# The first pair of heads in an attention and gated-MLP kernel: its loads on two queues and its parts made head by head

## The chip, the cores and the metric

The kernel runs on one core of a Trainium2 chip. The metric is the device time of one execution in microseconds (us). TensorE does the matrix products and the transposes, VectorE, ScalarE and GpSimd the elementwise work, and DMA transfers are issued here by the queue of SyncE (the sync queue).

## The reference

Attention over 2 batches of 12 heads, 448 positions, head size 64, then two layers on the 896 rows of 768 that come out of it.

```python
scores = scale * np.matmul(q, k.transpose(0, 1, 3, 2))     # causal mask, softmax
attn_out = np.matmul(attn, v)
x = attn_out.transpose(0, 2, 1, 3).reshape(B * S, H * D)
g = x @ w_gate                                             # 768 -> 1536
x = (g * sigmoid(g) * (x @ w_val)) @ w_out                 # 1536 -> 768
h = x @ w_in                                               # 768 -> 2048
out = (h * np.clip(h + 3, 0, 6) / 6) @ w2_out              # 2048 -> 768
```

The weights come as float64. The kernel makes float32 of them on the chip, and splits operands into a rounded high part and a remainder, so that the fast float32r products keep enough digits.

## The kernel before

Attention runs first, the two layers after it. Heads go in twelve pairs. For a pair, keys and queries are loaded as they lie (112 positions on the partitions, four chunks, two heads side by side), and `turn_parts` turns them on TensorE so that the 64 numbers of a position lie on the partitions: head 0 of the pair in rows 0 to 63, head 1 in rows 64 to 127. Scores are two products over 128 rows: one with the keys' high part (`kk`) in both halves, one with the keys' remainder (`k2`) in both halves, and the queries (`qq`) with their high part in one half and their remainder in the other. A turned half thus has to come into the other half as well. For pairs from the second on, ScalarE copies the turned block (L261), VectorE casts (L268), GpSimd makes the remainder (L269), and the sync queue copies each half of the keys to the other half by DMA (L274).

The first pair has a path of its own, `first_turn` (L278). Four transposes of the keys and four of the queries (L285), of both heads at once; then per head (`head`) two VectorE steps for the keys (L297, L298), ScalarE's cast of the queries (L299), a GpSimd and a ScalarE copy to the other half (L300, L302), and VectorE's remainder of the queries (L301). Head 0 is made at once, head 1 in the middle of round 0.

The rounds of L455 are one per head. Round t holds the scores and softmax of head t (`sc_parts`: products L330, VectorE L343, ScalarE L353), the transposes of the exponentials of head t-1 (`tp_parts`, L373), the value products of head t-2 (`pv_parts`, L401), and in even rounds the turns of the next pair, in odd ones the transposes of a finished pair. `weave` mixes the lists evenly. `busy(n)` puts n filler products on zeros (L194) on TensorE; the five numbers of `IDLE` (L31) say how many go where: at the start, behind the key transposes, behind the query transposes, in round 0, in round 1.

The order on an engine is not the written one throughout: a planner orders the instructions with costs of its own, in the written order where all is ready by its reckoning, and puts ready work ahead of work that it holds not ready. An instruction under `tc.keep_in_program_order` stays behind the one written before it on its engine; before, of TensorE's only the fillers do. Each engine then runs its list in order. Eight banks of PSUM are handed round by the list `idle`.

## Time and profile before

| | |
|---|---|
| median of 3 runs | 621.32 us (621.04 to 621.56) |
| the profiled execution | 619.02 us, span 617.2 us |
| TensorE busy | 607.9 us (98%), 3618 products |
| VectorE busy | 344.4 us (56%) |
| ScalarE busy | 264.7 us (43%) |
| GpSimd busy | 186.0 us (30%) |
| DMA | 70.15 MB, mean 114 GB/s |

The span runs from the first to the last instruction of the profiled execution; all positions below are microseconds from its start. PE is TensorE, PEld its weight load, DVE VectorE, ACT ScalarE, POOL GpSimd, SPq the sync queue. A product's length in the timeline includes its way through the array, so products that follow one another overlap; the distance of their starts is what each costs. L285 is line 285 of the kernel.

### The profile page before, as it was taken

Reading aid. Unit: us, or ns where it says so; the run is one execution under the profiler, and the core shown is the slowest. Engines: PE = TensorE matmul, PEld = TensorE weight load, DVE = VectorE, ACT = ScalarE, POOL = GpSimd, SP = SyncE. Lnnn points to the kernel's source line nnn. Section 1 sums busy time; section 2 is a strip of 40 time slices with the busy share of each in tenths; the row PEclk is TensorE's granted clock in tenths of the full one; section 3 lists DMA queues with packets and bytes.
Section 4 is the critical chain, followed back from the end, with each engine's and each line's share of the span. In section 5 each row is a group of like instructions: output and inputs, shape, how many; then the busy total and the mean of one; then the engine's idle time right before and its main releaser. Section 6 shows DMA issues by size and latency. Waiting matters only on the chain.

```text
span 617.2 us, 9392 instructions
## 1 busy us (share of the span) xinstructions
PE 607.9 (98%) x3618; PEld 561.8 (91%) x3618; DVE 344.4 (56%) x688; ACT 264.7 (43%) x450; POOL 186.0 (30%) x125
## 2 busy tenths in 40 slices
PE   8999998999999999999999999999999999999997
PEld 5999998988999988888999888889998899999996
DVE  6888889859854455554443444665656653325101
ACT  5687777744433333333323323555455532232100
POOL 4555665125222222222222222222222222213200
PEclk9999999999999999999999999999999999999999
DMA  9855543146443333333333333333343333352002
GB/s 184 226 138 132 138 110 97 58 150 201 157 125 127 108 102 103 102 103 103 117 124 115 105 103 102 104 102 108 111 132 111 102 103 103 102 180 65 0 4 88
DMA packets 83917, 70.15 MB, mean 114 GB/s; under 512 B 35232, under 2 KB 79776, under 8 KB 83872
## 3 DMA queue, kind: packets, MB, share of 16 engines
q1 hardware_dynamic: 83872, 69.55, 38.9%
q8 instruction: 29, 0.48, 0.3%
q14 instruction: 16, 0.13, 0.1%
HBM read 61.73 MB, written 2.75 MB: 104 GB/s over the span
## 4 chain that ended last, share of the span: by engine, by line
PE 94%; DVE 3%; ACT 1%; DMA 0%; issue 0%; SPq 0%; DVEq 0%; ACTq 0%
PE mm L170 60%; PE mm L547 19%; PE pv L401 5%; PE sc L330 4%; PE tp L373 3%; PE tr L255 1%; PE tr L435 1%; DVE e L343 1%; DVE qq L268 0%; DMA qn<-in_q_dram 0%; DVE w L102 0%; DVE w L105 0%; ACT e L353 0%; PE zero L194 0%; ACT whi L110 0%
## 5 line engine op out<-in xcount | busy, mean ns | idle before, releaser
L111 POOL TENSOR_TENSOR wlo<-w,whi 128x768 fp32r<-128x768 f32 x68 | 128.1, 1884 | 356.0 <-ACT whi L110 293.6
L101 DVE TENSOR_SCALAR w<-w 128x768 uint32<-128x768 uint32 x68 | 38.8, 570 | 155.9 <-ACT w L98 155.7
L110 ACT CAST whi<-w 128x768 fp32r<-128x768 f32 x68 | 56.9, 837 | 124.4 <-PE mm L170 82.8
L170 PE MATMUL mm<-x1l,whi 128*128 128x384 f32 (+1 forms) x288 | 104.9, 364 | 0.2 <-DVE x1l L153 0.2
L98 ACT ACTIVATE w<-raw 128x768 f32<-128x768 f32 x68 | 61.1, 898 | 102.1 <-POOL wlo L111 98.5
L170 PE MATMUL mm<-x1h,wlo 128*128 128x384 f32 (+1 forms) x288 | 104.9, 364 | 0.0
L170 PE MATMUL mm<-x1h,whi 128*128 128x384 f32 (+1 forms) x288 | 104.5, 363 | 0.0
L105 DVE SCALAR_TENSOR_TENSOR w<-raw,w 128x768 uint32<-128x768 uint32 x68 | 74.5, 1096 | 1.0
L547 PE MATMUL mm<-whi,gl 128*128 128x384 f32 x224 | 74.8, 334 | 0.0
L547 PE MATMUL mm<-whi,gh 128*128 128x384 f32 x224 | 74.8, 334 | 0.0
L547 PE MATMUL mm<-wlo,gh 128*128 128x384 f32 x224 | 74.8, 334 | 0.0
L401 PE MATMUL pv<-v,et 112*112 112x65 f32 x480 | 73.5, 242 | 0.0
L170 PE MATMUL mm<-x2h,wlo 128*128 128x384 f32 (+1 forms) x192 | 70.0, 364 | 0.0
L170 PE MATMUL mm<-x2l,whi 128*128 128x384 f32 (+1 forms) x192 | 69.8, 364 | 0.0
L170 PE MATMUL mm<-x2h,whi 128*128 128x384 f32 (+1 forms) x192 | 69.6, 362 | 0.0
L401 PEld LDWEIGHTS pv<-v,et 112*112 112x112 f32 x480 | 65.8, 177 | 1.2
L102 DVE SCALAR_TENSOR_TENSOR w<-raw,w 128x768 uint32<-128x768 uint32 x68 | 65.8, 968 | 1.6
L373 PE MATMUL tp<-ident,e 112*112 112x112 f32 x240 | 61.1, 261 | 3.1 <-ACT e L353 2.9
L170 PEld LDWEIGHTS mm<-x1l,whi 128*128 128x128 f32 x288 | 54.0, 188 | 6.5 <-DVE x1l L153 0.5
L170 PEld LDWEIGHTS mm<-x1h,whi 128*128 128x128 f32 x288 | 54.1, 188 | 6.2 <-ACT x1h L152 0.3
L170 PEld LDWEIGHTS mm<-x1h,wlo 128*128 128x128 f32 x288 | 54.0, 188 | 5.6
L353 ACT ACTIVATE e<-e,m 112x336 f32<-112x336 f32 (+1 forms) x96 | 48.6, 530 | 20.7 <-DVE m L343 20.6
(72 smaller groups left out, 1049.6 us busy)
## 6 DMA issues: line engine op xcount, KB each, us to landing
raw<-in_moe_w_out_dram SPq DMA_DIRECT2D x28, 768.0 KB, 4.3
raw<-in_moe_w_in_dram SPq DMA_DIRECT2D x16, 768.0 KB, 4.5
raw<-in_moe_w_gate_dram SPq DMA_DIRECT2D x12, 768.0 KB, 4.2
raw<-in_moe_w_val_dram SPq DMA_DIRECT2D x12, 768.0 KB, 4.3
kn<-in_k_dram SPq DMA_DIRECT2D x24, 112.0 KB, 2.8
qn<-in_q_dram SPq DMA_DIRECT2D x24, 112.0 KB, 2.7
v<-in_v_dram SPq DMA_DIRECT2D x12, 224.0 KB, 3.3
out_dram<-ob SPq DMA_DIRECT2D x14, 192.0 KB, 1.8
```

What stands on the lines that cost most here:

```text
L98: first = nc.scalar.activation(out=w, in_=high.bitcast(F32), func=AF.Copy, scale=2.0**-112)
L101: nc.vector.tensor_scalar(out=wu, in0=wu, scalar1=3, scalar2=None, op0=ALU.logical_shift_left)
L102: nc.vector.scalar_tensor_tensor(out=wu, in0=high, scalar=0x80000000, in1=wu, op0=ALU.bitwise_and, op1=ALU.bitwise_or)
L105: nc.vector.scalar_tensor_tensor(out=wu, in0=low, scalar=29, in1=wu, op0=ALU.logical_shift_right, op1=ALU.bitwise_or)
L110: nc.scalar.copy(hi, w)
L111: nc.gpsimd.tensor_tensor(out=lo, in0=w, in1=hi.bitcast(F32), op=ALU.subtract)
L170: lambda lhs=lhs, rhs=rhs, i=i: nc.tensor.matmul(ps, lhs, rhs, start=(first and i == 0), stop=(last and i == total - 1))
L330: nc.tensor.matmul(sp[:C, o : o + w], t["qq"][:, j, c * C : (c + 1) * C], t[("kk", "k2")[i]][:, j, 0:w], start=(i == 0), stop=(i == 1),)
L353: nc.scalar.activation(out=es, in_=es, func=AF.Exp, scale=-1.0, bias=m[:, x : x + 1])
L373: nc.tensor.transpose(tp[:C, at - lo : at - lo + C], e[:, at : at + C], ident[:C, :C])
L401: nc.tensor.matmul(box["o"][:, qc, :], et[:, at : at + C], vt[:, j, c, :], start=(c == 0), stop=(c == qc))
L547: nc.tensor.matmul(acc, lhs[:, tsl], rhs[:, i, :], start=(fc == 0 and n == 0), stop=(fc == K2 - 1 and n == 2),)
```

## The change

- Six loads take the place of `load(0)`: the keys of head 0 twice, side by side (`twice[0]`), the queries of heads 0 and 1, and the keys of head 1 twice. The first of each pair of loads goes to the sync queue, the other to ScalarE's queue. `load(1)` follows on the sync queue.
- The transposes are made head by head: keys 0, a filler, queries 0 (only the first 64 columns), a filler, queries 1, keys 1, two fillers: 16 transposes where there were 8. A transpose of doubled keys leaves them in both halves of its bank.
- Per head, ScalarE casts the keys for all 128 rows at once and VectorE makes their remainder for all 128; the copies to the other half are gone. The queries are made as before. Both heads are made ahead of round 0.
- Round 0 is written as the eight score products alone, then the eight turns of the second pair woven with three fillers. Round 1 begins with the first two score products of head 1; its other parts and two fillers are woven. The turns of the second pair and the scores of head 1 are kept in program order.
- `IDLE` goes from 6, 1, 3, 6, 2 to 5, 1, 1, 2, 3, 2.

```diff
-IDLE = (6, 1, 3, 6, 2)
+IDLE = (5, 1, 1, 2, 3, 2)
...
+                    if p == 1:
+                        tc.keep_in_program_order(turn)
...
             def first_turn():
                 t = sets[0]
-                got = {}
-                for nm, src in (("k", natk), ("q", natq)):
-                    got[nm] = bank("tr")
+                kb = [bank("tr") for _ in range(2)]
+                qb = [bank("tr") for _ in range(2)]
+
+                def keys(j):
                     for c in range(NC):
                         nc.tensor.transpose(
-                            got[nm][0][:, c * C : (c + 1) * C],
-                            src[0][:, c].rearrange("p j d -> p (j d)"),
+                            kb[j][0][:, c * C : (c + 1) * C],
+                            twice[j][:, c].rearrange("p j d -> p (j d)"),
                             ident[:C, :C],
                         )
-                    busy(IDLE[1] if nm == "k" else IDLE[2])
-                kt, qt = (got[nm][0][:, :S] for nm in "kq")
+
+                def queries(j):
+                    n = D * (j + 1)
+                    for c in range(NC):
+                        nc.tensor.transpose(
+                            qb[j][0][:n, c * C : (c + 1) * C],
+                            natq[0][:, c].rearrange("p j d -> p (j d)")[:, :n],
+                            ident[:C, :C],
+                        )
 
                 def head(j):
...
-                    nc.vector.tensor_copy(kk[r], kt[r])
-                    nc.vector.tensor_tensor(out=k2[r], in0=kt[r], in1=kk[r].bitcast(F32), op=ALU.subtract)
+                    kt, qt = (x[j][0][:, :S] for x in (kb, qb))
+                    nc.scalar.copy(kk, kt)
                     nc.scalar.copy(qq[r], qt[r])
-                    nc.gpsimd.tensor_copy(kk[o], kk[r].bitcast(F32))
+                    nc.vector.tensor_tensor(out=k2, in0=kt, in1=kk.bitcast(F32), op=ALU.subtract)
                     nc.vector.tensor_tensor(out=qq[o], in0=qt[r], in1=qq[r].bitcast(F32), op=ALU.subtract)
-                    nc.scalar.copy(k2[o], k2[r].bitcast(F32))
...
+                keys(0)
+                busy(IDLE[1])
+                queries(0)
+                busy(IDLE[2])
+                queries(1)
+                keys(1)
+                busy(IDLE[3])
                 head(0)
-                return [lambda: head(1)]
+                head(1)
...
+                    if n == 1:
+                        tc.keep_in_program_order(score)
...
-            load(0)
+            twice = [fix.tile([C, NC, 2, D], F32, name=f"twice{j}") for j in range(2)]
+            natq[0] = nat.tile([C, NC, 2, D], F32, tag="qn", name="qn")
+            def fetch(queue, dst, src):
+                queue.dma_start(out=dst, in_=src.rearrange("(c p) d -> p c d", p=C))
+            fetch(nc.sync, twice[0][:, :, 0, :], k[0, 0])
+            fetch(nc.scalar, twice[0][:, :, 1, :], k[0, 0])
+            fetch(nc.sync, natq[0][:, :, 0, :], q[0, 0])
+            fetch(nc.scalar, natq[0][:, :, 1, :], q[0, 1])
+            fetch(nc.sync, twice[1][:, :, 0, :], k[0, 1])
+            fetch(nc.scalar, twice[1][:, :, 1, :], k[0, 1])
             load(1)
             load_v(0)
-            second = first_turn()
+            first_turn()
...
-                fill = [lambda: busy(1)] * (IDLE[3 + t] if t < 2 else 0)
-                weave(sc_parts(t), tp_parts(t - 1), pv_parts(t - 2), turns_now, second, fill)
+                if t == 0:
+                    weave(sc_parts(t))
+                    weave(turns_now, [lambda: busy(1)] * IDLE[4])
+                    continue
+                fill = [lambda: busy(1)] * (IDLE[5] if t == 1 else 0)
+                scores = sc_parts(t)
+                if t == 1:
+                    weave(scores[:2])
+                    scores = scores[2:]
+                weave(scores, tp_parts(t - 1), pv_parts(t - 2), turns_now, fill)
```

## Rows read from the trace of the kernel before

**Rows 1.** busy time by stretch (start:end, length; per engine busy, instructions; then clock, DMA)
```profile
7.89:10.81 2.92, 1.77 (x12) 1.36 (x11) 2.67 (x10) 2.19 (x6) 2.25 (x2) 1.00 1.35 214
...
14.05:18.60 4.55, 4.55 (x44) 4.46 (x45) 2.83 (x12) 3.29 (x8) 2.08 (x2) 1.00 0.99 266
18.60:27.50 8.90, 8.80 (x88) 8.48 (x87) 7.62 (x29) 6.32 (x15) 5.08 (x5) 1.00 0.87 220
```

**Rows 2.** waits of TensorE over the span (us in total, times, longest)
```profile
PE tp L373 <- ACT e L353: 2.9, 3, 1.6
```

**Rows 3.** timeline of TensorE (start, length, what, idle before and its releaser)
```profile
1.19 2.74 PE L194 MATMUL zero<-zeros 128*128 128x512 bf16 x6 [1.19 <-DVE half L523]
3.72 0.76 PE L285 MATMUL tr<-ident,kn 112*128 112x112 f32 x4
...
5.11 0.57 PE L285 MATMUL tr<-ident,qn 112*128 112x112 f32 x4 [0.41 <-DMA qn<-in_q_dram]
5.52 0.81 PE L194 MATMUL zero<-zeros 128*128 128x512 bf16 x3
6.17 0.29 PE L255 MATMUL tr<-ident,kn 112*128 112x112 f32 x1
...
7.89 0.38 PE L330 MATMUL sc<-kk,qq 128*112 128x336 f32 x1
...
10.81 0.31 PE L373 MATMUL tp<-ident,e 112*112 112x112 f32 x1 [1.15 <-ACT e L353]
...
14.05 0.31 PE L373 MATMUL tp<-ident,e 112*112 112x112 f32 x1 [0.20 <-ACT e L353]
...
14.65 0.39 PE L330 MATMUL sc<-k,qq 128*112 128x336 f32 x1
```

**Rows 4.** timeline of VectorE
```profile
4.51 0.62 DVE L297 CAST kk<-tr 64x448 fp32r<-64x448 f32 x1 [3.34 <-PE tr L285]
...
7.13 0.62 DVE L301 TENSOR_TENSOR qq<-tr,qq 64x448 fp32r<-64x448 f32 x1
8.01 0.81 DVE L268 CAST kk<-f 64x448 fp32r<-64x448 f32 x2 [0.26 <-ACT f L261]
...
10.06 0.27 DVE L343 CUSTOM_DVE_ANT_0 e<-sc,mask 112x112 f32<-112x112 f32 x1
```

**Rows 5.** chain of work that ended last (start, length on the chain)
```profile
8.06 0.80 PE sc L330 x6
...
14.53 0.10 PE tr L255
14.63 0.16 PE pv L401 x2
```

**Rows 6.** timeline of the sync queue
```profile
0.74 0.92 SPq L229 DMA_DIRECT2D kn<-in_k_dram  x2
```

**Rows 7.** DMA landings of issues in 0:1.1, 2.2:2.3 and 9.8:9.9
```profile
kn<-in_k_dram SPq DMA_DIRECT2D x1, 112.0 KB, 2.3
...
qn<-in_q_dram SPq DMA_DIRECT2D x1, 112.0 KB, 2.7
...
k<-k SPq DMA_DIRECT2D x1, 112.0 KB, 3.4
```

**Rows 8.** busy time by stretch, 2 to 3 us
```profile
2.00:3.00 1.00, 1.00 (x4) 0.43 (x3) 0.00 (x0) 0.01 (x1) 0.04 (x2) 1.00 0.89 202
```

**Rows 9.** timeline of ScalarE
```profile
0.73 1.28 ACT L299 ACT_TABLE_LOAD   x1 [0.73 <-PEq L591]
...
7.45 0.53 ACT L261 COPY f<-tr 128x448 f32<-128x448 f32 x1 [0.62 <-PE tr L255]
```

**Rows 10.** VectorE by shape, 20:210 (count, busy us, mean ns)
```profile
L153 DVE TENSOR_TENSOR x1l<-tr,x1h 128x448 fp32r<-128x448 f32 x12 | 7.4, 616 | 1.4 <-ACT x1h L152 1.3
```

**Rows 11.** VectorE by line, 4.4 to 14.05 us
```profile
L343 DVE CUSTOM_DVE_ANT_0 e<-sc,mask 112x336 f32<-112x336 f32 (+3 forms) x8 | 3.3, 447 | 0.4 <-PE sc L330 0.3
```

**Rows 12.** timeline of GpSimd
```profile
8.48 2.56 POOL L269 TENSOR_TENSOR k<-f,kk 64x448 fp32r<-64x448 f32 x2 [1.43 <-DVE kk L268]
```

More of the change, by code (lines that the diff above doesn't have):

```diff
@@ L254, in one @@
                     tr, bn = box["tr"]
-                    nc.tensor.transpose(
+                    turn = nc.tensor.transpose(
                         tr[:, c * C : (c + 1) * C], n[:, c].rearrange("p j d -> p (j d)"), ident[:C, :C]
                     )
+                    if p == 1:
+                        tc.keep_in_program_order(turn)
                     if c < NC - 1:
@@ L296, in head @@
                     kk, k2, qq = (t[nm][:, j, :] for nm in ("kk", "k2", "qq"))
-                    nc.vector.tensor_copy(kk[r], kt[r])
-                    nc.vector.tensor_tensor(out=k2[r], in0=kt[r], in1=kk[r].bitcast(F32), op=ALU.subtract)
+                    kt, qt = (x[j][0][:, :S] for x in (kb, qb))
+                    nc.scalar.copy(kk, kt)
                     nc.scalar.copy(qq[r], qt[r])
-                    nc.gpsimd.tensor_copy(kk[o], kk[r].bitcast(F32))
+                    nc.vector.tensor_tensor(out=k2, in0=kt, in1=kk.bitcast(F32), op=ALU.subtract)
                     nc.vector.tensor_tensor(out=qq[o], in0=qt[r], in1=qq[r].bitcast(F32), op=ALU.subtract)
-                    nc.scalar.copy(k2[o], k2[r].bitcast(F32))
-                    if j == 1:
-                        idle.extend(n for _, n in got.values())
+                    idle.extend((kb[j][1], qb[j][1]))
+                keys(0)
[5 more added lines that the diff above has]
+                busy(IDLE[3])
                 head(0)
-                return [lambda: head(1)]
+                head(1)
             def sc_parts(n):
@@ L329, in product @@
                     sp, bn = box["sp"]
-                    nc.tensor.matmul(
+                    score = nc.tensor.matmul(
                         sp[:C, o : o + w],
@@ L463, in attention @@
                     turns_now = xt_parts((t - 5) // 2)
-                fill = [lambda: busy(1)] * (IDLE[3 + t] if t < 2 else 0)
-                weave(sc_parts(t), tp_parts(t - 1), pv_parts(t - 2), turns_now, second, fill)
+                if t == 0:
[8 more added lines that the diff above has]
+                weave(scores, tp_parts(t - 1), pv_parts(t - 2), turns_now, fill)
                 if t == 1:
                     idle.append(idler[1])
-                second = []
                 if t in UNIT_AT:
```

## The prediction

> **What bounds the kernel now.** I read the busy time by stretch first [rows 1]. From 14.05 us TensorE has no free time (4.55 of 4.55 us), and it keeps 8.80 of the next 8.90; before that it is free for 1.15 of 2.92 us (7.89 to 10.81). So the end of the program is set by when TensorE gets through its first round of work, and from then on by TensorE's own work, which this change leaves alone. The list of TensorE's waits says the same: 2.9 us in three waits for the exponentials [rows 2]; one of them is the 1.15 us before 10.81 [rows 3]. The order of TensorE shows the start: six filler products, four key transposes at 3.72, a wait of 0.41 us for the queries, four query transposes at 5.11, fillers, the first scores at 7.89, the first transpose of exponentials at 10.81, and that of the second head at 14.05 [rows 3]. Between them VectorE stands on the chain: it starts at 4.51 and takes four halves of the first pair at 0.65 us each before 7.13, and the product that releases 10.81 comes only at 10.06, behind work for the second pair (8.01) and the second head [rows 4]. From the end of that product (10.33) to the transpose there are 0.48 us, ScalarE's exponential.
>
> My yardstick is therefore one state of TensorE: scores of both heads done, the eight second-pair transposes done, the first head's ten exponential transposes and one value product done. Before, that state is reached at 14.05. The gain is how much earlier it comes, less any wait that the third round then gets.
>
> **The change, part by part.**
>
> *Loads.* Two issues of 112 KB take 0.92 us on the sync queue [rows 6], so 0.46 each. The first lands 2.3 us after its issue, the queries 2.7 [rows 7]. A load issued by ScalarE's queue is in no row here. Bounds: if two queues run side by side, the three pairs (keys 0, queries, keys 1) are issued at 0.74, 1.2 and 1.7 and land at 3.1, 3.9 and 4.4; if they count as one line, the second of each pair is issued at 1.2, 2.2 and 3.2 and lands at 3.6, 4.9 and 5.9. The bytes speak for the later end: 202 GB/s between 2 and 3 us with the 16 engines 89% busy [rows 8], and six pieces are 688 KB, 3.4 us at that rate. I take 3.55, 4.65 and 5.8. The table load of 1.28 us that now opens ScalarE's list [rows 9] belongs to its first cast; I put it behind the three issues, where it ends by 3.5 and hides under the loads. If it stays first, ScalarE's issues start at 2.0 and the keys land at 4.4, some 0.4 us off the gain.
>
> [...]
>
> *First head.* Five fillers instead of six: six take 3.72 - 1.19 = 2.53 us, 0.42 each [rows 3], so TensorE is free at 3.3 and the keys wait for their load until 3.55. Four transposes take 0.76 to their result: 4.3. ScalarE casts all 128 rows at once; 128x448 takes it 0.53 [rows 9], 0.55 with the gap: 4.35 to 4.9. Keys loaded twice side by side leave the transpose with both halves filled, so the copies by GpSimd and ScalarE (two each) go; VectorE loses its two casts, 2 x 0.65 = 1.3 us. Its subtraction for the remainder is now 128 rows; 128x448 takes 0.616 [rows 10], so as much as 64 rows. Queries of head 0: 4.65 + 0.57 = 5.2; ScalarE 5.25 to 5.8; VectorE's remainder 5.85 to 6.5. On TensorE's list ahead of the scores stand queries and keys of head 1 (four transposes each, 0.10 a piece [rows 5]), ready at 5.8 + 0.4 = 6.2, and two fillers at 0.215 (three in a row take 0.65 of pace in the row at 5.52 [rows 3]): 6.65. The scores start at 6.65, not 7.89. The eight added transposes (0.8 us) and the four fillers saved (18 become 14) stand in this time.
>
> *Second head and first softmax.* ScalarE has queries 1 from 5.8 and keys 1 from 6.4 to 6.95; VectorE 6.5 to 7.15 and 7.15 to 7.8. Now come the first head's softmax products, eight of which took 3.3 us for two heads, 0.45 each [rows 11]. The first transpose needs two, 8.7, and with 0.48 of exponential it could run at 9.2, against 10.81.
>
> *TensorE's list meanwhile.* Eight scores are 0.80 + 0.40 = 1.2 us [rows 5]: 7.85. The second pair's turns with three fillers: 0.8 + 0.65 = 1.45: 9.3. Two scores of head 1: 0.4: 9.7. The rest of that round: six scores 0.8, ten transposes 1.0, two fillers 0.43, one value product 0.16: 12.1. VectorE needs four more products and the 0.81 of the second pair's casts [rows 4] before the second head's transposes: 8.7 + 1.8 + 0.8 = 11.3, with the exponential 11.8, so TensorE is later. The state of 14.05 comes at 12.1, or at 12.5 if the copies of the transposes stand ahead on VectorE; I take 12.3, a gain of 1.75 us.
>
> *What is late next.* The second pair's turns are now behind the scores. Their key transposes end at about 8.6 instead of 7.45, where ScalarE copied them [rows 9]. That copy queues behind the first head's four exponentials unless the planner slips it in: it ends between 9.4 and 10.75, before at 7.98. From the copy to the landed second half of the keys' remainder it took 7.98 to 13.26: cast 0.4, GpSimd 1.28 (two in 2.56 [rows 12]), the issue and 3.4 to landing [rows 7]. The same 5.25 us puts it now at 14.65 to 16.0. The third round's second score product needs it; before it ran at 14.65 [rows 3], with over a microsecond to spare. Now the spare is gone. The cover is other work of that round: nine value products at 0.16, ten transposes and eight turns at 0.10 [rows 5], 3.2 us from 12.3 to 15.5. These are not held in program order, and the planner moves such work: before, it set second-pair turns ahead of the first scores (the one at 6.17 [rows 3] is the first of six). Full cover leaves at most 16.0 - 15.5 = 0.5 us; as the planner goes by its own costs and may bring too little forward, I charge 0.35. Bounds: nothing (copy at 9.4, landed inside the cover), and the whole gain and more (nothing moved, first rival).
>
> Sum: 1.75 - 0.35 = 1.4 us earlier. The profiled execution took 619.02 us with a span of 617.2, 1.8 around it; it would take 617.6, with a span of 615.8. The median of the runs is 621.32, 2.3 above it; the same difference gives 619.9.
>
> **Rivals.**
>
> 1. *The third round stands in order (slower).* If the planner believes the copied halves landed, it leaves the third round as written, and TensorE waits at the second score product until 14.65 to 16.0, against 14.65 before: 0 to 1.35 us lost, 0.7 in the middle, 622.0. It decides as soon as the copy of the turned keys starts later than 8.85. For it: that round ran in exactly the written order before. Against: it was ready then, and at 10.81 TensorE's list was rearranged around exponentials that were not.
> 2. *Two queues act as one.* Keys 1 land at 6.0 and the scores start at 6.85; VectorE gets its last half 0.25 us later. Gain 1.15: 620.2. The change then still saves VectorE's casts. For it: 0.46 us per issue is back to back in the row. Against: nothing shown.
> 3. *Two queues are fully parallel.* Loads at 3.1, 3.9 and 4.4; the scores wait for VectorE alone and start at about 6.1. Gain 2.0: 619.3. Against: the bytes [rows 8].
> 4. *VectorE is the bound.* It is 7.62 of 8.90 us busy after 18.60 [rows 1]. If TensorE gets ahead and VectorE only by its 1.3 us less the 0.45 by which it starts later and a gap of 0.25, the gain is 0.6: 620.7. Against: VectorE was free 1.7 us between 14.05 and 18.60.
>
> **How the numbers follow.** Chances: forecast 0.45 (its own spread 619.2 to 620.6), rival 1 0.15, rival 2 0.13, rival 3 0.15, rival 4 0.12. About 0.2%, 1.24 us, is what a measurement of this kernel can tell from no change, so faster means below 620.08, which the forecast is in 6 of 10 cases. Faster: 0.28 + 0.14 + 0.05 and 0.03 from the rest, 0.50. Slower than 622.56: a part of rival 1 and mishaps, 0.08. Same: 0.42. Range 618.8 to 622.0: it leaves out the late half of rival 1 and the tails.
>
> **What would show it.** Right: ScalarE issues three loads before its table load; first scores at 6.5 to 6.9; no VectorE cast before the first remainder; the first exponential transpose near 9.7; value products of the third round ahead of its scores. Wrong: a table load ahead of ScalarE's issues; keys later than 3.7; a TensorE wait of over 0.5 us between 12 and 16 us for scores; VectorE without a pause from 5 to 23 us while TensorE waits for exponentials.

## The result and the profile after

The changed kernel takes 624.87 us in the median of 6 runs (624.54 to 626.17), the kernel before 621.18 in the same comparison (6 runs, 618.5 to 622.39). The ratio is 1.0067, with a 95% interval of 1.0046 to 1.0089: slower by 3.7 us, where 619.9 was forecast. Executions of one kernel spread over 2 to 5 us here, and most of that goes with TensorE's mean granted clock: of the kernel before those at 0.999 to 1.0 took some 618 to 619 us, with a few up to 621, those at 0.994 some 621 to 623. Where it matters, medians are therefore compared as ratios within one comparison, and the executions at the same granted clock beside them.

| | before | after |
|---|---|---|
| profiled execution | 619.02 us, span 617.2 | 626.17 us, span 624.4 |
| TensorE busy | 607.9 us | 612.8 us |
| VectorE, ScalarE, GpSimd busy | 344.4, 264.7, 186.0 us | 344.0, 264.4, 184.5 us |
| DMA | 70.15 MB | 70.38 MB |

First, from the page of after, TensorE's granted clock in 40 slices (15.6 us each).

```profile
PEclk9899999799999999999999999999999999999999
```

The 9s have two dents that mean lost clock, in the second slice and in the eighth. The timeline of TensorE (start, length, what, idle before and its releaser) answers to [rows 3]:

```profile
1.19 2.31 PE L195 MATMUL zero<-zeros 128*128 128x512 bf16 x5 [1.19 <-DVE half L560]
3.92 0.94 PE L289 MATMUL tr<-ident,twice 112*128 112x112 f32 x4 [0.41 <-DMA twice<-in_k_dram]
...
6.26 0.60 PE L289 MATMUL tr<-ident,twice 112*128 112x112 f32 x4 [0.19 <-DMA twice<-in_k_dram]
...
6.95 0.50 PE L346 MATMUL sc<-kk,qq 128*112 128x336 f32 x1
...
10.01 0.26 PE L391 MATMUL tp<-ident,e 112*112 112x112 f32 x1
...
12.17 0.26 PE L391 MATMUL tp<-ident,e 112*112 112x112 f32 x1
14.33 0.38 PE L419 MATMUL pv<-v,et 112*112 112x65 f32 x2 [1.90 <-DVE et L397]
14.86 0.41 PE L391 MATMUL tp<-ident,e 112*112 112x112 f32 x1 [0.15 <-ACT e L371]
17.63 0.59 PE L346 MATMUL sc<-kk,qq 128*112 128x336 f32 x1 [2.36 <-DMA kk<-kk]
...
24.18 0.38 PE L346 MATMUL sc<-kk,qq 128*112 128x336 f32 x1
```

Two more rows of TensorE before, the first score products of the third and the fourth round:

```profile
14.15 0.38 PE L330 MATMUL sc<-kk,qq 128*112 128x336 f32 x1
...
18.79 0.38 PE L330 MATMUL sc<-kk,qq 128*112 128x336 f32 x1
```

Up to 12.17 us the change does what was expected. The scores start at 6.95 us, not 7.89, and the first transpose of exponentials runs at 10.01, not 10.81. From there to 17.63 TensorE runs only the transpose at 12.17, two value products and one more transpose, and stands for most of the rest: 1.90 us for VectorE, 2.36 for a copy by DMA. The first score product of the third round comes at 17.63 (14.15 before), that of the fourth at 24.18 (18.79 before): 3.5 us, then 5.4. Between the two starts lie 6.55 us, 4.64 before: the waits are followed by a lower clock. The busy time by stretch (start:end, length; per engine busy and instructions; then granted clock, DMA share, GB/s):

```profile
12.17:14.33 2.16, 0.26 (x3) 0.03 (x1) 2.07 (x6) 0.34 (x2) 2.08 (x2) 1.00 1.17 274
...
16.00:18.00 2.00, 0.37 (x1) 0.39 (x2) 0.00 (x0) 0.20 (x1) 0.00 (x0) 0.50 1.15 215
18.00:20.00 2.00, 2.00 (x12) 1.94 (x11) 0.64 (x3) 0.24 (x1) 0.00 (x0) 0.50 1.30 210
20.00:22.00 2.00, 2.00 (x15) 2.00 (x14) 0.38 (x1) 0.78 (x2) 0.00 (x0) 0.56 0.90 304
...
112.00:116.00 4.00, 4.00 (x22) 3.71 (x21) 1.83 (x10) 1.65 (x4) 0.51 (x1) 0.50 0.31 108
```

The granted clock is 0.50 from 16 to 20 us, and TensorE is fully busy from 18 us on. A second-pair transpose of that stretch takes 0.19 us of the chain (18.22), one at 22.11 takes 0.10. The last row is the other dent: 112 to 116 us, behind a wait of 1.56 us for exponentials in the 22nd round, which the kernel before has as well (ending at 103.89, 1.56 us; in after at 109.01). The profiled execution of the kernel before kept the clock there; in the profile of its variant with four opening fillers (below) it reads 0.50 from 108 to 112 us.

Who was late is seen on the other queues of the same profile. The timeline of VectorE:

```profile
10.22 0.81 DVE L271 CAST kk<-f 64x448 fp32r<-64x448 f32 x2 [0.66 <-ACT f L264]
...
11.49 2.04 DVE L271 CAST qq<-f 64x448 fp32r<-64x448 f32 x2
13.56 0.51 DVE L397 COPY et<-tp 112x336 f32<-112x336 f32 x1
```

The same casts of the queries before:

```profile
11.92 0.81 DVE L268 CAST qq<-f 64x448 fp32r<-64x448 f32 x2
```

The timeline of GpSimd in after:

```profile
10.69 2.59 POOL L272 TENSOR_TENSOR k<-f,kk 64x448 fp32r<-64x448 f32 x2 [8.65 <-DVE kk L271]
```

And that of its sync queue:

```profile
0.74 0.39 SPq L474 DMA_DIRECT2D twice<-in_k_dram  x1
...
5.49 1.52 SPq L230 DMA_DIRECT2D kn<-in_k_dram  x2
7.06 1.63 SPq L240 DMA_DIRECT2D v<-in_v_dram  x2
8.81 1.57 SPq L230 DMA_DIRECT2D qn<-in_q_dram  x2
10.42 0.67 SPq L95 DMA_DIRECT2D raw<-in_moe_w_gate_dram  x1
11.19 0.88 SPq L230 DMA_DIRECT2D kn<-in_k_dram  x1
12.17 0.52 SPq L277 DMA_DIRECT2D kk<-kk  x1
```

Before, the first weight load went out behind the copies (the first of them at 8.95):

```profile
13.95 0.56 SPq L94 DMA_DIRECT2D raw<-in_moe_w_gate_dram  x1
```

VectorE has the first half of the turned keys at 10.61 (10.22 and half of 0.81). The copy of that half is issued at 12.17 only, because the queue is then at a weight load of 768 KB (10.42), with a piece of keys for a later pair (11.19) still to go. Since 5.49 it has issued almost without a pause, and slowly: 1.5 us and more for two, where [rows 6] has 0.92. Two transfers stand ahead of the copies that went out behind them before: the weights and one load of values (13.42 before). And it lands late. The landing of that issue (form, count, size, us from issue to landing), beside 3.4 in [rows 7]:

```profile
kk<-kk SPq DMA_DIRECT2D x1, 112.0 KB, 5.3
```

The chain of work that ended last goes through it, from 12.17 to the third round:

```profile
12.17 5.32 DMA kk<-kk
```

### The profile page after: what moved, and what is told of

Its sections match the earlier page's. It is cut to its first block, busy times and chain, and to the rows that moved or that the text cites. A ratio compares the mean times of both kernels' runs of the same rounds, so it can differ in the third digit from the quotient of the medians.

```text
span 624.4 us, 9393 instructions
## 1 busy us (share of the span) xinstructions
PE 612.8 (98%) x3621; PEld 567.1 (91%) x3622; DVE 344.0 (55%) x686; ACT 264.4 (42%) x450; POOL 184.5 (30%) x123
## 2 busy tenths in 40 slices
DMA packets 84845, 70.38 MB, mean 113 GB/s; under 512 B 36160, under 2 KB 80704, under 8 KB 84800
## 4 chain that ended last, share of the span: by engine, by line
PE 95%; DVE 2%; DMA 2%; ACT 1%; issue 0%; ACTq 0%; DVEq 0%
PE mm L171 59%; PE mm L584 19%; PE pv L419 6%; PE sc L346 5%; PE tp L391 4%; PE tr L256 1%; DMA kk<-kk 1%; DMA twice<-in_k_dram 1%; PE tr L453 1%; DVE w L103 0%; DVE e L361 0%; DVE w L106 0%; DVE qq L271 0%; ACT e L371 0%; ACTq L474 0%
## 5 line engine op out<-in xcount | busy, mean ns | idle before, releaser
L419 PE MATMUL pv<-v,et 112*112 112x65 f32 x480 | 76.1, 248 | 1.9 <-DVE et L397 1.9
L419 PEld LDWEIGHTS pv<-v,et 112*112 112x112 f32 x480 | 68.7, 185 | 3.7 <-issue 2.2
L391 PE MATMUL tp<-ident,e 112*112 112x112 f32 x240 | 63.0, 268 | 1.8 <-ACT e L371 1.7
```

The source lines that it names most:

```text
L391: nc.tensor.transpose(tp[:C, at - lo : at - lo + C], e[:, at : at + C], ident[:C, :C])
L419: nc.tensor.matmul(box["o"][:, qc, :], et[:, at : at + C], vt[:, j, c, :], start=(c == 0), stop=(c == qc))
```

## Experiments

Eighteen kernels ran. "Before" is the kernel before's median in the same comparison.

| run | median, us | before | ratio (95%) |
|---|---|---|---|
| weight load behind the copies | 624.73 | 619.87 | 1.0071 (1.0046 to 1.0096) |
| turns ahead of scores | 621.98 | 619.87 | 1.0036 (1.0018 to 1.0054) |
| third round's scores last | 626.92 | 619.87 | 1.0112 (1.0082 to 1.0142) |
| fillers in the third round | 624.34 | 619.87 | 1.0074 (1.0046 to 1.0102) |
| before, seven fillers in round 22 | 619.97 | 620.14 | 0.9994 (0.9979 to 1.0010) |
| after, seven fillers in round 22 | 625.2 | 620.14 | 1.0077 (1.0051 to 1.0104) |
| second pair made like the first | 623.04 | 620.14 | 1.0041 (1.0020 to 1.0062) |
| queries' casts on ScalarE | 625.52 | 620.14 | 1.0081 (1.0058 to 1.0104) |
| transfers behind the copies | 622.97 | 619.71 | 1.0055 (1.0037 to 1.0073) |
| the same, casts on ScalarE | 621.55 | 619.71 | 1.0025 (1.0009 to 1.0042) |
| the same, turns ahead too | 621.47 | 619.71 | 1.0021 (1.0001 to 1.0041) |
| before, loads split | 621.48 | 619.71 | 1.0020 (1.0000 to 1.0040) |
| after, seven opening fillers | 626.47 | 620.64 | 1.0100 (1.0073 to 1.0127) |
| before, four opening fillers | 622.08 | 620.64 | 1.0029 (1.0011 to 1.0047) |
| transfers, casts, seven opening | 621.84 | 620.64 | 1.0023 (1.0001 to 1.0045) |
| the same, turns ahead too | 620.03 | 620.64 | 1.0002 (0.9983 to 1.0020) |
| corrected, none in round 22 | 620.15 | 620.1 | 1.0006 (0.9985 to 1.0027) |
| corrected, four in round 22 | 619.23 | 620.1 | 0.9986 (0.9970 to 1.0002) |

### Where TensorE stands

**Weight load behind the copies**

```diff
+        with tc.issue_after(copies[-1].ins):   # the second pair's last copy
             nc.sync.dma_start(out=raw..., in_=src)
```

> The changed kernel, but the first weight load is held behind the four copies of the second pair's keys on the sync queue (in the changed kernel it is issued at 10.42 us, ahead of the first copy at 12.17, which lands only at 17.6). Theory A (the copies are late, and the 768 KB in front of them make a good part of it): first copy issued near 11.6 and landed near 15.5, the wait for it 0.3 to 1 us instead of 2.4, 622.5 to 623.5. Rival B (the copies wait for ScalarE, VectorE and GpSimd, the bytes in front cost nothing): same landing, within 0.3 us of the changed kernel's 624.9.

TensorE's timeline (the last row is the fourth round's first score), the landing of the copy issued at 11.53, and the busy time from 16 to 20 us:

```profile
14.41 0.38 PE L423 MATMUL pv<-v,et 112*112 112x65 f32 x2 [2.08 <-DMA kn<-in_k_dram]
...
15.73 0.59 PE L350 MATMUL sc<-kk,qq 128*112 128x336 f32 x1 [0.48 <-DMA kk<-kk]
...
23.33 0.39 PE L350 MATMUL sc<-kk,qq 128*112 128x336 f32 x1
```

```profile
kk<-kk SPq DMA_DIRECT2D x1, 112.0 KB, 4.1
```

```profile
16.00:20.00 4.00, 4.00 (x24) 3.93 (x23) 1.02 (x3) 1.20 (x3) 0.00 (x0) 0.50 0.94 242
```

The copy is issued at 11.53 and lands in 4.1 us. The wait for it shrinks to 0.48 us, and the third round's scores start 1.9 us earlier than in after. The wait ahead of the value product stays (2.08 us; the releaser named in its row is a load, but in after and in the run with the scores last it is VectorE), and the clock is at 0.50 from 16 to 20 us all the same. So the fourth round starts only 0.85 us earlier (23.33 against 24.18). The two executions at 0.994 and 0.995 took 622.4 and 622.8 us, 2 us below those of after at that clock (624.5); the other four, at 0.991 and 0.992, took 624.7 to 625.2, those of after at 0.992 625.1 and 625.8. The median, 624.73, is not shown to differ from after's and misses theory A's range. So the queue is a cause of the late third round; what that is worth at the end lies between nothing and 2 us, as the clock takes it back or not.

**Turns ahead of the first scores**

```diff
-                    weave(sc_parts(t))
                     weave(turns_now, [lambda: busy(1)] * IDLE[4])
+                    weave(sc_parts(t))
```

> The changed kernel, but the second pair's turns and their three fillers are written ahead of the first head's scores, the part 'turns behind the scores' undone; the planner then also puts the first weight load behind the copies. Theory A: the turned keys are copied by ScalarE near 7.6 instead of 9.7, the copies are issued near 9 and landed by 13.3, no wait for them; the third round starts at 13.5 to 14.5 and the time is 620 to 621.5, as before or a little less. Rival B (what costs is VectorE and ScalarE having both heads of the first pair ahead of the first softmax): third round no earlier than 15, 623 or more.

No wait for a copy is left, and no loss of clock before 100 us. The longest wait is now 1.67 us for exponentials at 14.74. The execution profiled had a late start (scores behind turns that begin at 8.79), so its copies, at 11.60, are not earlier than those of the run before. Of after's 0.67% about half is left, with two things changed at once: the weight load, too, goes out behind the copies here (16.05). The median lies 0.5 us above the range that theory A gave.

**The third round's scores last**

```diff
+                if t == 2:
+                    weave(tp_parts(t - 1), pv_parts(t - 2), turns_now)
+                    weave(scores)
+                    continue
```

> The changed kernel, but in the third round the scores are written behind all its transposes, value products and turns. Theory A: the wait of 2.4 us for the copies goes, since 3.2 us of other work stands in front of them; TensorE keeps its clock there, 620.5 to 622. Rival B (VectorE is late anyway, the wait only changes its name): another wait of 1.5 us or more shows in the third or fourth round, 623.5 to 625.

Its list of TensorE's waits (us in total, times, longest):

```profile
PE tp L391 <- ACT e L371: 3.6, 3, 1.9
PE pv L419 <- DVE et L397: 2.0, 1, 2.0
```

The wait for the copies is gone, but the wait for exponentials grew to 3.6 us: 1.92 of it at 23.31, in the round after, with a clock of 0.60 from 24 to 28 us. Bringing all of the round's other work forward was no gain: the scores, put last, are late for the next softmax. A part of it alone was not tried.

**Fillers in the third round**

```diff
+                if t == 2:
+                    busy(9)
+                    pvs[0]()
+                    tps[0]()
+                    busy(11)
```

> The changed kernel, with 9 filler products on TensorE ahead of the third round's first value product and 11 ahead of its first score product, 20 at 0.215 us = 4.3 us, put where TensorE stands for 1.9 and 2.4 us. Theory C (the clock fell to the lower level because TensorE stood, and that costs about 2 us of the loss): granted clock 1.00 through the third round, its length 4.5 us instead of 6.5, 622.5 to 623.3. Rival (the clock falls with or without fillers, or its fall costs little): 624.5 to 625.5.

The busy time from 16 to 20 us, and the first scores of the third and the fourth round:

```profile
16.00:20.00 4.00, 4.00 (x29) 2.78 (x30) 0.89 (x4) 1.25 (x3) 0.77 (x1) 1.00 1.23 208
```

```profile
18.61 0.40 PE L346 MATMUL sc<-kk,qq 128*112 128x336 f32 x1
...
23.09 0.38 PE L346 MATMUL sc<-kk,qq 128*112 128x336 f32 x1
```

The clock stays at 1.00 through the third round, which takes 4.48 us, against 6.55 in after: there the lower clock cost about 2 us, as theory C had it. The median, 624.34, is above its range all the same; the three executions at 0.993 to 0.995 took 625.5 to 626.0, and in the profile of one of them the clock falls near 110 us. Executions at 0.999 took 622.8 and 623.1, those of before at 0.999 to 1.0 took 618.1 to 619.1: some 4 us without the clock's fall in the third round. Part of that can be the fillers, which hold TensorE themselves, so this run bounds the loss from the waits and does not measure it.

### The fall near 110 us, and VectorE

The next four share a change: seven fillers at the head of the 22nd round, ahead of the wait of 1.56 us.

**Before, with them**

```diff
+                if t == 21:
+                    busy(7)
```

> The kernel before, with 7 filler products (1.5 us) written at the head of the 22nd round, where TensorE stands for 1.56 us at 102 us in its profile. The runs of the kernel before lie between 618.1 and 623.0 with granted clocks of 0.999 down to 0.991. Theory C (after that wait the clock falls in some executions, and a fall costs 3 to 4 us): runs close together at 618 to 619.5, clock 0.998 or more, median 618.8. Rival (the spread has another place): spread as before, median within 0.5 us of the kernel before.

Ten of twelve executions are at 0.999 or 1.0 and between 619.2 and 620.1; of the kernel before alone 9 of 24 are at 0.994, at 621.0 to 623.1. So the fall near 110 us makes most of its spread. The fillers cost about 1 us, since its own executions at full clock took 618.3 to 619.3, but for two of 620.0 and 620.7.

**After, with them**

> The changed kernel with the same 7 fillers in the 22nd round. Theory C: what is left against the kernel before with the fillers is the third round alone: 3.5 us of later scores and some 2 us of lower clock there, so 5 us above it, 622.5 to 624, clock 0.994 to 0.996. Rival (the late clock falls come from that second place): 620.5 to 622.

This kernel is the twin that the later expectations speak of. One execution kept 1.0 throughout (622.45), the others lay at 0.994 to 0.997 (624.1 to 626.5), and the median, 625.2, is above the expected 624: the third round still takes its clock. That one is 2.4 to 3.2 us above before's ten.

**Second pair made like the first** (keys loaded twice, casts of 128 rows by ScalarE, remainders by VectorE, no copies)

```diff
+                        nc.scalar.copy(t["kk"][:, j], x)
+                        nc.vector.tensor_tensor(out=t["k2"][:, j], in0=x, in1=t["kk"][:, j].bitcast(F32), op=ALU.subtract)
```

> The changed kernel with the fillers of the 22nd round, and the second pair made as the first is: its keys loaded twice side by side, 128-row casts on ScalarE and remainders on VectorE, no GpSimd step and no copy by DMA. Theory A (the copies and the steps that feed them are the loss): no wait at the third round's scores, which start near 13; 617 to 618.5, below both kernels. Rival B (with these steps on them, ScalarE and VectorE are the bound): third round at 14 to 15, 618.5 to 620.

TensorE's timeline, the one long wait:

```profile
14.78 0.43 PE L377 MATMUL sc<-kk,qq 128*112 128x448 f32 x1 [1.98 <-DVE qq L307]
```

Without any copy by DMA the clock holds in the third round, and the executions at 0.999 and 1.0 take 620.5 to 621.8. The remaining wait, 1.98 us in the second round, is for VectorE, which now makes the remainders itself. The third round starts late all the same (16.04), and the median, 623.04, is above both theories.

**Queries' casts on ScalarE**

```diff
-                        nc.vector.tensor_copy(hi[r, j, :], f[r, :])
+                        (nc.scalar.copy if p == 1 and src is natq else nc.vector.tensor_copy)(hi[r, j, :], f[r, :])
```

> The changed kernel with the fillers of the 22nd round, and the high parts of the second pair's queries cast by ScalarE, not by VectorE, whose two casts took 2.04 us beside GpSimd's subtraction (0.81 before). Theory A (the copies of the keys gate the third round): the first value product comes at 12.5 to 13 instead of 14.33, but the scores still wait for the copies until 17 to 17.6, time within 0.5 us of the changed kernel with the fillers. Rival B (VectorE's lateness is the loss): scores earlier by 1 us or more and time lower by as much.

TensorE's timeline:

```profile
17.65 0.59 PE L347 MATMUL sc<-kk,qq 128*112 128x336 f32 x1 [3.23 <-DMA kk<-kk]
```

The value product waits no more (12.73), and the first score of the third round starts at 17.65, as in after. The wait for the copy is 3.23 us instead of 2.36. So VectorE's casts are a second, shorter wait, hidden behind the copies: removed alone they give nothing.

### Both causes away

**Transfers behind the copies** (the weight load as above, and)

```diff
+                    if t == 2:
+                        with tc.issue_after(copies[-1].ins):
+                            load_v(nxt - 1)
+                            load(nxt + 1)
+                            load_v(nxt)
```

> The changed kernel with the second and third pairs' values, the fourth pair's parts and the first weight load all issued behind the second pair's key copies, and seven fillers in the 22nd round so that the clock fall near 110 us stays out. Theory A (the third round stands for the key copies, which stand in the sync queue behind transfers nobody needs yet): the first copy is issued at 10.9 to 11.6 instead of 12.17, it lands in 3.4 to 4 us, the third round's first score product starts at 15.0 to 15.8 (17.63 to 17.92 in the changed kernel and in its twin with the seven fillers); TensorE's wait for a copy falls under 1 us; 621.5 to 622.5 us in the median, 2.5 to 3.5 below that twin. The value product still waits for VectorE at 14.3 to 15.7. Theory B (the waits only change their name): the value product, or an exponential of the fourth round, takes over and the median stays at 624 to 625.

The timeline of the sync queue, and the landing of the first copy:

```profile
7.48 0.89 SPq L233 DMA_DIRECT2D qn<-in_q_dram  x2
12.32 0.53 SPq L280 DMA_DIRECT2D kk<-kk  x1
```

```profile
kk<-kk SPq DMA_DIRECT2D x1, 112.0 KB, 2.1
```

The queue is empty from 8.4 us on, and the copy goes out as soon as the cast allows. It lands in 2.1 us: 5.3 in after, 4.1 with the weight load alone out of the way. The median is 3.3 us above before's, where the twin's was 5.1 above (the intervals of the two ratios overlap); at a clock of 1.0 the two executions here (622.2 and 622.3) are level with the twin's one (622.45). The third round's first score starts at 16.66, with no wait for the copy, and the value product still waits 1.68 us for VectorE, as expected. The copy itself was issued later than expected, since this execution's scores started at 8.49.

**The same, with the casts on ScalarE**

> As the run with the transfers behind the copies, and ScalarE instead of VectorE makes the high parts of the second pair's queries, so that VectorE's 2.04 us of casts beside GpSimd are away. Theory A with both causes: no wait for a value product at 14.3; the first score product of the third round at 14.7 to 15.5; the remainder of the keys (GpSimd from about 11.2, 1.28 us a half, issue, 3.4 us to landing) holds the second score product until about 16, against 14.65 before; 620.0 to 621.5 us, 0.5 to 1.5 above the kernel before. Theory B: the median stays within 1 us of the run with the transfers alone.

The median is 1.8 us above before's, so now the casts seem to count, by 1.4 us (the intervals of the two runs still touch). With both causes away, 1.8 of the twin's 5.1 us are left, and here the intervals of the ratios (up to 1.0042, from 1.0051) are apart. The third round's first score starts at 16.06, later than expected, with the first scores at 8.35.

**The same, with the turns ahead**

> As the run with both causes away, and the second pair's turns with their three fillers written ahead of the first scores, as the kernel before had most of them. Theory A (what counts is when the second pair's copies start): ScalarE's copy of the turned keys at 8.6 to 9.5 instead of 9.7 to 10.2, copies issued from 9.8 to 10.6, no wait of TensorE for a copy over 0.5 us; the first scores come 1.3 us later (8.2); the third round's first score product at 14.2 to 15.0; 618.8 to 620.5 us, the same as the kernel before. Theory B: the later start of the scores costs what the earlier copies give, 621 to 622.5 as turns ahead alone (621.98).

No further gain, as theory B had it: 621.47 in the median, with executions from 619.5 to 623.8.

**Before, with the first pair's loads split**

```diff
-                        nc.sync.dma_start(
+                        (nc.scalar if p == 0 and src is q else nc.sync).dma_start(
```

> The kernel before with one piece of the change alone: the first pair's queries are issued by ScalarE's queue while the sync queue issues its keys; and the seven fillers in the 22nd round. If the split of the loads has a worth by itself: the queries land some 0.5 us sooner, TensorE's wait of 0.41 us at 5.11 goes, and the median is 0.2 to 0.4 below the kernel before with the fillers alone (619.97), so 619.6 to 619.8. If VectorE's four steps of 0.65 us stand on the chain anyway: no difference, 619.9 to 620.1. If the shared engines make the keys land later: up to 0.5 us slower.

Slower than every theory had it: 621.48, a ratio of 1.0020, where the kernel with the fillers alone had 0.9994 (the intervals overlap). Its profile points to the third theory's reason. The keys come later: issued beside the queries, they have their transposes at 4.67, after a pause of 0.73 us for the load (3.72 and none before); and TensorE's fillers keep a pace of 0.43 us each up to 9.3 us. Not every execution pays: at a clock of 1.0 four took 619.6 to 619.7, as the kernel with the fillers alone, and four 620.9 to 622.1, the profiled one among them.

### The opening

TensorE's fillers of 512 columns start 0.425 us apart at first and 0.215 apart later, a ratio of two: in after the four key transposes at 3.92 come 0.19 us apart, those of the queries at 4.92 0.10, and at 18 us, where the granted clock reads 0.50, a transpose costs 0.19 again. The granted clock does not show the slow opening (it reads 1.00 there), the distances do. In the kernel before, whose fillers reach the keys without a pause, the pace has changed by 4.3 us (by 5.8 in its run with fillers in round 22). In eleven profiles of kernels with five opening fillers, which pause 0.41 to 0.64 us for the keys, it changes anywhere between 4.7 and over 9 us.

**After, with seven opening fillers**

```diff
-IDLE = (5, 1, 1, 2, 3, 2)
+IDLE = (7, 1, 1, 2, 3, 2)
```

> The changed kernel with seven opening fillers for five, nothing else. Theory (the pause ahead of the key transposes keeps TensorE at its lower level): fillers end at 4.2, no wait for the doubled keys, spacing 0.215 from about 5 us on, first scores at 7.0 to 7.3. The third round still waits for the copies of the second pair, which the sync queue issues at about 12.2 whatever TensorE does, so little of it arrives: 623.5 to 624.8 us (624.87 with five). Rival (the rise is chance): the profile may show either, and the median stays at 624.5 to 625.2.

TensorE's timeline:

```profile
6.98 0.50 PE L346 MATMUL sc<-kk,qq 128*112 128x336 f32 x1
...
18.13 0.59 PE L346 MATMUL sc<-kk,qq 128*112 128x336 f32 x1 [2.76 <-DMA kk<-kk]
```

The pause went and the pace changed early, but the kernel did not become faster: 1.0100 times before, where after was 1.0067 (the intervals overlap), and all executions lie at 0.988 to 0.992. Neither theory had that. In the profiles the scores start no earlier (6.98 against 6.95, since the pace changed early in after's profile as well), and the second head's first transpose stands at 14.93 against 14.86. The copy is issued later (12.45, in after 12.17), and the product that waits for it starts 5.68 us behind the issue (5.46 in after), so TensorE stands 2.76 us for it. So this run can't tell the worth of the pause: the copy hides it.

**Before, with four opening fillers**

```diff
-IDLE = (6, 1, 3, 6, 2)
+IDLE = (4, 1, 3, 6, 2)
```

> The kernel before with four opening fillers for six, nothing else: a pause of about 0.85 us ahead of the key transposes, which don't start earlier. Theory: the spacing of 0.215 comes at 8 us or later instead of 4.3 to 5, first scores at 8.9 to 9.3 instead of 7.89, 0.8 to 1.5 us slower: 620.5 to 621.5 beside about 619.7. Rival: no difference within 0.3 us, because VectorE's chain of four halves sets the scores in any case.

TensorE's timeline:

```profile
3.91 0.98 PE L285 MATMUL tr<-ident,kn 112*128 112x112 f32 x4 [0.83 <-DMA kn<-in_k_dram]
...
8.86 0.51 PE L330 MATMUL sc<-kk,qq 128*112 128x336 f32 x1
...
11.99 0.31 PE L373 MATMUL tp<-ident,e 112*112 112x112 f32 x1 [1.23 <-ACT e L353]
```

The pause (0.83 us) makes the scores start at 8.86 instead of 7.89 and the first transpose of exponentials at 11.99 instead of 10.81. The price is 1.4 us in the median, and 2 us at a clock of 0.999 (620.3 and 620.6; before 618.0 to 618.4, but for one of 620.8). The fillers are no mere cover.

**Transfers, casts, and seven opening fillers**

> The changed kernel with the transfers behind the copies, the queries' casts on ScalarE and the seven fillers in the 22nd round (621.55 with five opening fillers), now with seven opening fillers. Theory: turns of the second pair at 8.4 instead of about 9.6, ScalarE's copy of the turned keys at about 10.1 instead of 11.2, the third round's first score product at 14.9 instead of 16.06; 620.3 to 620.8 us, 0.8 to 1.2 less. Rival: no difference, 621.3 to 621.8.

**The same, with the turns ahead**

> The same with the second pair's turns ahead of the first scores (621.47 with five opening fillers), now with seven. Theory: the slow openings go, all executions stand where the fastest stood (619.5 to 620.4), median 619.7 to 620.3; that is no more than the kernel before with the seven fillers in the 22nd round (619.97). Rival: the wait for exponentials near 11.5 (0.97 us, VectorE's softmax) takes up what comes earlier, 621.0 to 621.5.

The first misses: 621.84, a ratio of 1.0023, 1.0025 with five. Its profile shows the expected early start (third round at 14.50), but a clock of 0.84 and 0.73 from 12 to 20 us. The second does what was expected: 620.03, level with before (1.0002; 1.0021 with five).

**Corrected, with none and with four fillers in round 22** (transfers behind the copies, casts on ScalarE, turns ahead, seven opening fillers)

> The corrected kernel (turns ahead, transfers behind the copies, casts on ScalarE, seven opening fillers) without the fillers in the 22nd round. If those seven fillers cost the 1 us: executions at full clock at 617.8 to 618.4, as the kernel before; the others, after a clock fall near 110 us, at 619.5 to 622; median within 0.7 us of the kernel before. If something of the change is left: full-clock executions stay at 619.0 or above and the median is 1 us or more above before.

> The same with four fillers in the 22nd round in place of seven. If the price goes with their number and four already keep the clock: 618.4 to 619.0 at full clock, in most executions, median 618.6 to 619.4, 1 us or 0.2% below the kernel before. If four don't keep the clock: the spread of the kernel without them, median 620 to 621.

TensorE's timeline in the corrected kernel without fillers in round 22:

```profile
8.80 0.39 PE L350 MATMUL sc<-kk,qq 128*112 128x336 f32 x1
...
11.45 0.59 PE L395 MATMUL tp<-ident,e 112*112 112x112 f32 x3 [0.98 <-ACT e L375]
...
14.19 0.39 PE L350 MATMUL sc<-kk,qq 128*112 128x336 f32 x1
...
18.83 0.38 PE L350 MATMUL sc<-kk,qq 128*112 128x336 f32 x1
```

At full clock the corrected kernel takes 618.6 to 619.5 us, before 618.3 to 618.7 (but for two of 619.1 and 621.2). In its profile the third and the fourth round's first scores stand at 14.19 and 18.83: before at 14.15 and 18.79. With everything repaired, the two-queue loads and the doubled keys bring TensorE to the same place at the same time, because the turns had to go back ahead of the scores (8.80 instead of 6.95) and the transposes then wait 0.98 us for exponentials. With four fillers in round 22 nothing is at 0.994 any more, and the median, 619.23, is the lowest of all; its interval reaches 1.0002, so it is not shown to beat the kernel before. Even here the pace of one profiled opening changed only near 7.2 us with no pause (the query transposes at 6.50 come 0.185 us apart, the key transposes at 7.24 0.095), so a late change does not need the pause. One wait is left open: in the profiles of the corrected kernel with seven and with four fillers in round 22 TensorE stands 1.3 us (up to 42.22) and 1.1 us (between 24 and 100 us) for a key copy, a wait that the kernel before doesn't have; without the fillers it doesn't show.

## Why the prediction was wrong

- **Loads** a little too early. The keys' transposes ran at 3.92 (forecast 3.55; "later than 3.7" was a sign of being wrong), keys 1 at 6.26 (5.8 for the load). Rivals 2 and 3 are out: the two queues issue side by side, and the loads land later than fully parallel ones would (3.1 for the keys). By its times alone rival 2 (keys 1 at 6.0, scores at 6.85) came nearer than the forecast, but not for its reason.

  The timeline of ScalarE in after:

```profile
0.73 0.42 ACTq L474 DMA_DIRECT2D twice<-in_k_dram  x1
...
2.32 1.28 ACT L309 ACT_TABLE_LOAD   x1 [2.32 <-issue]
...
9.68 0.51 ACT L264 COPY f<-tr 128x448 f32<-128x448 f32 x1
```

  ScalarE's first issue, at 0.73, takes 0.42 us beside the sync queue's first, at 0.74, of 0.39; the two after it run beside theirs too, and the table load comes behind all three. With one queue alone an issue took 0.46 before.
- **First head, softmax** nearly right, 0.3 us late: scores 6.95 (6.65), first transpose 10.01 (9.7). TensorE's list was through by 12.17 (12.1), but for the value product and the second head's first transpose, which VectorE held until 14.33 and 14.86 (11.8). So the yardstick state of 14.05 came at 14.86, 0.8 us later than before and not 1.75 earlier. That much is rival 4, in one place.
- **What is late next** is the step that failed: 0.35 us were charged for it, and TensorE stood 4.3 (1.90 and 2.36). It failed in three terms. *The copies' start:* ScalarE's copy of the turned keys ended at 10.19, inside the forecast 9.4 to 10.75, but from there I took 5.25 us as before, to 15.5. To the landing of the first copy, for which the first score product stood, it took 7.3 us, to 17.5 (before 5.0, 7.98 to 12.95); to that of the remainder, the one I had counted, 7.7, to 17.9. The sync queue was put down as free; but the copies come later, and loads of later pairs and the weights stand ahead of them (the weights and one load of values went out behind them before): 1.56 us on the queue and 5.3 us to landing. I had read [rows 6] and [rows 7] for the duration of an issue, not for what would stand in the queue by then. *VectorE:* the sum has 0.81 us of casts once, for the keys [rows 4]; they took that again (10.22). The casts of the queries came ahead of the second head's softmax too, beside GpSimd's subtraction, and took 2.04 us for two. The subtraction was already running then (10.69 to 13.28); before, the same casts took 0.81, and it began only at 12.38. ScalarE's casts of the same halves in the casts run took 1.16 beside it, about as much as two of its 0.53 with their gap. What makes VectorE's casts longer there is not shown. *The cover:* none of the 3.2 us of other work was brought forward. That is rival 1, the third round in written order, to which I gave 0.15; the run with the scores last shows that bringing the whole cover forward costs in the next round.
- **The size of rival 1** was wrong too: 622.0, worked out from a wait of 0 to 1.35 us. It was 4.3 us with the value product's, and the sum had no term for what comes after: the granted clock at 0.50 up to some 21.7 us (0.62 on average from 21 to 22; 1.9 us more between the third and fourth round's delays).
- **The opening** was counted at a filler saved (18 to 14). No term was there for the pace at which TensorE runs when it pauses before the keys; four for six in the kernel before cost 1.4 us in the median. In after's profile the pace changed early (4.7 us), so this is no part of the delays above; in other executions of after it may be.

What is shown: the queue makes the copy late (its landing takes 5.3, 4.1 and 2.1 us as transfers leave its way), VectorE's casts give nothing while it is not clear, both together make most of the loss (1.0077 to 1.0025), and four opening fillers for six, with a pause of 0.83 us, cost the kernel before 1.4 us. What is not settled is the share of each, and of the clock, in after's 3.7 us: the queue alone moved no median clear of noise, and the runs that kept the clock (fillers, 622.8 and 623.1) added work of their own.

## What to carry to other kernels

Before a transfer on the critical path is moved later, list what its queue will hold by then: loads that used to go out behind it can come to stand ahead of it, and with them there it can land later (here 5.3 us after its issue, 2.1 with them out of the way). A gain at the head of a pipeline counts only up to the first hand-over that did not move with it; follow each product of a moved step to its last consumer. And where the granted clock falls behind a wait of TensorE, the wait costs more than its own length (here some 2 us more: the third round took 6.55 us with the clock at 0.50 up to 21.7 us, 4.48 with the clock at 1.00).

## What was unexpected in the hardware

- A 112 KB copy within SBUF landed 2.1 us after its issue where no DMA moved at that time (0 GB/s from 12.3 to 12.4, transfers behind the copies), 2.8 (the first) and 2.2 us (the last) in the corrected kernel, 4.0 before (the first), and 5.3 in after (the first), where DMA moved 215 to 350 GB/s from 12.17 to 18 us.
- Two VectorE casts of 64x448 took 0.81 us before and 2.04 where GpSimd's subtraction was already running.
- Two more opening fillers in after, with no pause left before the keys, gave nothing back: TensorE stood longer for the copy (2.76 us), and the mean clock of the six executions was 0.988 to 0.992 (after 0.989 to 0.995).
- The granted clock reads 1.00 from 1 to 8 us in the profiles of both kernels and of the first twelve runs of the table, while fillers start 0.42 us apart up to 3.7 us in the kernel before, still 0.43 at 8.7 in the run with the loads split, and 0.215 later.
